# Wider w_out products and a corrected planner in a fused attention and two-expert kernel

## The chip, the cores and the metric

The kernel runs on one core of a Trainium2 chip. The metric is device time in microseconds (us), the median of three runs. Its engines are TensorE (PE in the profile; PEld is its weight load), VectorE (DVE), ScalarE (ACT), GpSimd (POOL) and SyncE (SP), whose queue starts the DMAs.

## The reference

Four batches, eight heads, 576 positions, head size 64. Keys and values are pooled into 32 memory slots by a softmax over positions; queries attend to the 32 slots. The result, 2304 tokens by 512 columns, goes through two multilayer parts.

```python
a = softmax(phi, axis=2)                       # over positions
k_m = einsum('bhsm,bhsd->bhmd', a, k)
v_m = einsum('bhsm,bhsd->bhmd', a, v)
attn = softmax(q @ k_m.T / sqrt(64))           # over the 32 slots
x = (attn @ v_m) as 2304 x 512
h = x @ w_in                                   # 512 x 2048
x = (h * sigmoid(1.702 * h)) @ w_out           # 2048 x 512
xn = x / sqrt(mean(x*x) + 1e-6) * rms_g
g = xn @ w_gate; val = xn @ w_val              # 512 x 1536 each
out = (silu(g) * val) @ w_o2                   # 1536 x 512
```

Weights of the two parts are float64; their 64-bit words are turned into float32 on the chip.

## The kernel before

**Numbers.** Every large product is made of three: high times high, low times high, high times low. The high half is a value rounded to the type fp32r that TensorE takes, the low half (made by `sub_lo`, line 680) is what the rounding left.

**Stages.** The batches form two pairs; a pair has 1152 tokens. Attention units (batch, half of the heads) make transposed scores `attnT` with the names pk, pq. The first part, "a", runs in 16 groups: 2 pairs by 8 slices of 256 hidden columns. For a group, `vm_part` (line 1017) multiplies the pooled values into w_in, so that `a_g1` (line 1055) gets the hidden columns directly from the attention weights. A step of `a_g1` covers 288 tokens; it makes two tiles `gr`, one for each 128 hidden columns: six products into a PSUM tile, the gelu on ScalarE (`gf`), a cast to the high half on ScalarE, and a subtraction for the low half on GpSimd or DVE. `a_g2` (line 1082) multiplies these by w_out: for each of four blocks of 128 output columns six products, and the sum is added into `x` by DVE (copied by ScalarE in the first group of a pair). After that come the norm (`norm_1` to `norm_4`) and the second part, "b", in 6 groups of 256 columns, with 384 tokens in a step (`b_g3` with w_gate and w_val, `b_g4` with w_o2). Loops run over groups outside and token steps inside; attention of the second pair and the norm steps are put in between as side work.

**Weights.** `w_load` (line 696) brings 1024 32-bit words a partition into one of three `raw` tiles. `w_conv` (line 714) makes float32 in a tile `pad` (part a) or `cv` (part b): an absolute value on ScalarE, a clamp (`tensor_scalar` with max and min), a shift, two merges, all on DVE unless a table says otherwise; then the cast to the high half, and the subtraction to the low half. For the second pair the float32 comes back from a cache in DRAM.

**What sets the order.** No engine's order is written by hand. All operations are recorded, and a planner (`Plan.order`, line 474) simulates the engines with a duration for every operation (`cost`, line 346) and a rate for loads (in `order`), and sends each engine's operations in the order of that simulation. Two tables bend it. `HASTE` gives a step an earlier or later due time. `OTHER` names operations of a step, by their number within it, that move from DVE to GpSimd or back. Where the simulation leaves TensorE idle, it writes products of a tile of ones (`fill`, line 557) that nobody reads; in the rows they are products with `ones_r` of 512 columns. All the recorded operations are issued at one line, 586, so rows are told apart by their tiles.

**Buffers.** Pools have a set number of buffers: `cv` 6 for float32 work, `gp` 5 for `gr`, `pp`, `sr` and `rb`, `km` 2 for `kz` and `vz`, 4 `kmT`, 8 PSUM banks. `spare` buffers are kept for the norm steps.

Of the kernel before, what the change touches and what calls it, by code (L numbers as in the profile page):

```python
# [116 lines left out]
class Plan:  # L117
# [10 lines left out]
        "a_g1 0 2 2": 34.2,  # L128
        "a_g1 0 3 0": -35.6,
        "a_g1 0 6 2": 17.9,  # L130
        "a_g1 1 3 2": 57.3,
        "a_g1 1 3 3": 40.2,
        "a_g1 1 6 3": 24.6,
        "a_g1 1 7 0": 28.0,
        "a_g1 1 7 2": 17.0,
        "a_g2 0 0 3": 35.8,
        "a_g2 0 2 3": -19.2,
        "a_g2 0 3 1": 7.7,
        "a_g2 1 0 2": 41.3,
        "a_g2 1 1 1": 41.2,  # L140
        "att_k1 3 0": 35.9,
        "att_k3 3 0": 20.5,
        "att_k4 2 1": 32.9,
        "att_k4 3 0": 7.4,
        "att_k5 1 0": 58.0,
        "att_k5 2 0": -36.4,
        "att_q1 2 0 0": 22.5,
        "att_q1 2 1 1": 15.0,
        "att_q3 2 0 0": 20.7,
        "att_q3 3 0 0": -0.9,  # L150
        "att_q3 3 1 1": 52.4,
        "att_q3s 2 1 0": -28.4,
        "att_q3s 2 1 1": 11.8,
        "att_q3s 3 0 1": 17.9,
        "att_q4 1 1 0": 54.2,
        "att_q4 2 0 1": -9.3,
        "att_q4 3 0 1": -11.3,
        "b_g3 0 2": 6.4,
        "b_g3 1 0": 34.5,
        "b_g3 1 4": -15.0,  # L160
        "b_g3 1 5": 4.6,
        "b_g4 5 4": -96.5,
        "ld_src 0 0 1": 46.6,
        "norm_2 0 2": 23.2,
        "norm_3 0 1": 22.5,
        "norm_4 0 0 2": 28.2,
        "norm_4 0 1 0": -19.0,
        "norm_4 0 1 3": 5.2,
        "norm_4 1 1 1": 26.5,
        "vm_part 0 1 1 0": 19.0,  # L170
        "vm_part 0 3 0": 18.6,
        "vm_part 0 3 1": 19.5,
        "vm_part 0 6 0": 29.2,
        "vm_part 0 7 0": 37.3,
        "vm_part 0 7 1": 17.5,
        "vm_part 1 1 0": 41.6,
        "vm_part 1 3 1": 50.7,
        "w_conv a 0 4 in 1": 40.2,
        "w_conv a 0 5 out 0": 41.1,
        "w_conv a 1 7 in 0": 67.8,  # L180
        "w_conv b 0 o2 0": 20.1,
        "w_conv b 0 val 0": 28.6,
        "w_load a 0 4 out 0": 57.5,
        "w_load b 0 o2 0": 34.1,
# [1253 lines left out]
```

## Time and profile before

| | |
|---|---|
| median of 3 runs | 885.97 us (885.95 to 886.06) |
| profiled execution | 885.36 us, of which the span from first to last instruction is 883.6 |
| TensorE busy | 865.5 us (98%), 5826 products |
| DVE, ScalarE, GpSimd busy | 553.5, 409.4, 279.6 us |
| granted TensorE clock, mean | 0.995 |
| chain that ended last | TensorE 82%, most of it products into the PSUM tiles pg (77%) |

A row of a timeline has its start, its duration, the engine, the operation, the tiles (out<-in, without buffer numbers), the shape and how many such instructions are merged; in brackets stands how long the engine was idle before, and what released it. The tiles pg hold the results of `a_g1`, `a_g2`, `b_g3` and `b_g4` alike. Products are pipelined, so the duration of a single one holds its latency; the distance between two starts is what it costs in a stream. A granted clock of 1.00 is 2.4 GHz, one of 0.5 is 1.2 GHz.

### The profile page before, as it was taken

To read this page: it belongs to the slowest core of one execution; us is meant where nothing else is said; L and a number is where in the kernel's file an instruction comes from. 1 tells how busy PE (TensorE), PEld (TensorE's weight loads), DVE (VectorE), ACT (ScalarE), POOL (GpSimd) and SP (SyncE) were. 2 spreads that over 40 slices of the span, in tenths; PEclk is the share of its full clock that TensorE was granted. 3 is DMA by queue.
4 is the path that set the end of the run, shared out by engine and by line. 5 is a ranking of instruction groups with operands and counts; after the bars stand their busy time and mean duration, and the time that the engine had idled before them with its cause. 6 is when DMAs were issued, how large, how long until landed. Compare 5 with 4: busy or idle time off the path is not lost.

```text
span 883.6 us, 14955 instructions
## 1 busy us (share of the span) xinstructions
PE 865.5 (98%) x5826; PEld 823.5 (93%) x5826; DVE 553.5 (63%) x1113; ACT 409.4 (46%) x891; POOL 279.6 (32%) x262
## 2 busy tenths in 40 slices
PE   7999989999999999999999999999999999999997
PEld 5889989999999999999999999999999999999997
DVE  4979889998964378688876563194366346333333
ACT  2687658677767656565574531231132132111110
POOL 2254565455485755664250110210021021001000
PEclk9999999999999999999999999999999999999999
DMA  9975548755411212122322040022022000000214
GB/s 237 265 183 142 154 150 228 197 143 150 117 52 42 72 30 66 50 84 75 100 69 92 0 144 1 1 74 70 1 71 73 1 1 24 1 1 1 61 48 108
DMA packets 40535, 74.64 MB, mean 84 GB/s; under 512 B 3856, under 2 KB 16144, under 8 KB 40464
## 3 DMA queue, kind: packets, MB, share of 16 engines
q1 hardware_dynamic: 40464, 73.68, 30.2%
q8 instruction: 46, 0.75, 0.4%
q14 instruction: 25, 0.20, 0.1%
HBM read 60.56 MB, written 13.11 MB: 83 GB/s over the span
## 4 chain that ended last, share of the span: by engine, by line
PE 82%; DVE 2%; DMA 1%; ACT 1%; issue 0%; DVEq 0%; SPq 0%
PE pg L586 77%; PE pvm L586 2%; PE pq L586 1%; DMA kmisc<-in_phi_dram 1%; PE pk L586 1%; DVE kmisc L586 0%; PE pnm L586 0%; DVE stage L586 0%; PE pnr L586 0%; DVE gr L586 0%; DVE x L586 0%; DVE vm_7l L586 0%; ACT L586 0%; ACT vm_6h L586 0%; DVE pad L586 0%
## 5 line engine op out<-in xcount | busy, mean ns | idle before, releaser
L586 PE MATMUL pg<-gr,a_outh 128*128 128x288 f32 x960 | 207.0, 297 | 2.8 <-POOL gr L586 1.3
L586 PEld LDWEIGHTS pg<-gr,a_outh 128*128 128x128 f32 x960 | 158.3, 188 | 4.5 <-DVE gr L586 2.3
L586 PE MATMUL pg<-gr,a_outl 128*128 128x288 f32 x480 | 141.2, 294 | 1.3 <-DVE a_outl L586 1.3
L586 PE MATMUL pg<-b_o2h,pp 128*128 128x512 f32 x432 | 140.7, 391 | 0.0
L586 DVE TENSOR_TENSOR x<-x,pg 128x288 f32<-128x288 f32 x224 | 97.8, 449 | 52.4 <-PE pg L586 50.6
L586 DVE TENSOR_TENSOR pf<-sg,pg 128x384 f32<-128x384 f32 x72 | 39.9, 554 | 144.8 <-PE pg L586 132.8
L586 ACT ACTIVATE sg<-pg 128x384 f32<-128x384 f32 x72 | 35.3, 491 | 152.1 <-PE pg L586 150.3
L586 PEld LDWEIGHTS pg<-b_o2h,pp 128*128 128x128 f32 x432 | 81.1, 188 | 16.0
L586 ACT CAST pp<-pf 128x384 fp32r<-128x384 f32 x72 | 37.0, 513 | 126.4 <-DVE pf L586 126.0
L586 POOL TENSOR_TENSOR gr<-gf,gr 128x288 fp32r<-128x288 f32 x82 | 71.2, 877 | 72.4 <-ACT gr L586 58.2
L586 POOL TENSOR_TENSOR b_o2l<-cv,b_o2h 128x512 fp32r<-128x512 f32 x10 | 12.8, 1299 | 253.4 <-ACT b_o2h L586 217.6
L586 PEld LDWEIGHTS pg<-gr,a_outl 128*128 128x128 f32 x480 | 90.2, 188 | 1.5 <-DVE a_outl L586 1.5
L586 DVE TENSOR_TENSOR oacc<-oacc,pg 128x512 f32<-128x512 f32 x90 | 61.7, 685 | 44.3 <-PE pg L586 43.8
L586 PE MATMUL pg<-b_o2l,pp 128*128 128x512 f32 x216 | 84.7, 392 | 0.0
L586 ACT ACTIVATE gf<-pg 128x288 f32<-128x288 f32 x128 | 51.9, 410 | 36.8 <-PE pg L586 35.5
L586 PE MATMUL pg<-xnh,b_gateh 128*128 128x384 f32 x288 | 62.0, 336 | 0.0
L586 PE MATMUL pg<-xnh,b_gatel 128*128 128x384 f32 x288 | 61.8, 335 | 0.0
L586 PE MATMUL pg<-xnh,b_valh 128*128 128x384 f32 x288 | 61.6, 334 | 0.0
L586 PE MATMUL pg<-xnh,b_vall 128*128 128x384 f32 x288 | 61.5, 334 | 0.0
L586 PE MATMUL pg<-xnl,b_valh 128*128 128x384 f32 x288 | 61.5, 334 | 0.0
L586 PE MATMUL pg<-xnl,b_gateh 128*128 128x384 f32 x288 | 61.5, 334 | 0.0
L586 ACT CAST gr<-gf 128x288 fp32r<-128x288 f32 x128 | 53.7, 433 | 16.7 <-PE pg L586 8.7
(210 smaller groups left out, 1777.9 us busy)
## 6 DMA issues: line engine op xcount, KB each, us to landing
raw_a_in<-in_moe_w_in_dram SPq DMA_DIRECT2D x16, 512.0 KB, 5.3
raw_a_out<-in_moe_w_out_dram SPq DMA_DIRECT2D x16, 512.0 KB, 5.0
cache<-pad SPq DMA_DIRECT2D x32, 256.0 KB, 4.9
raw_b_gate<-in_moe_w_gate_dram SPq DMA_DIRECT2D x12, 512.0 KB, 3.8
raw_b_val<-in_moe_w_val_dram SPq DMA_DIRECT2D x12, 512.0 KB, 3.7
raw_b_o<-in_moe_w_out_dram SPq DMA_DIRECT2D x12, 512.0 KB, 3.8
stage<-in_k_dram SPq DMA_DIRECT2D x8, 576.0 KB, 7.8
stage<-in_v_dram SPq DMA_DIRECT2D x8, 576.0 KB, 9.4
```

The costliest lines, as they stand in the source:

```text
L586: getattr(self.real[op.eng], op.name)(*op.args, **op.kw)
```

## The change

**w_out products.** A step of `a_g2` covers 384 tokens in place of 288, except in the first two groups of the first pair. The steps of `a_g1` keep 288 tokens, so a `gr` tile of 384 tokens is now filled by two of them: a new function, `pieces`, cuts a step of `a_g1` at the borders of the 384-token tiles. Steps 1 and 2 of a group make two pieces each, of 96 and 192 tokens, each with its own cast and its own subtraction. The loop over slots sends a step of `a_g2` one slot after the one that completed its tile.

```diff
+    def width(pr, g):
+        return HALF if (pr, g) in ((0, 0), (0, 1)) else TB
+
+    def pieces(pr, g, t):
+
+        w, a = width(pr, g), t * HALF
+        while a < (t + 1) * HALF:
+            k = a // w
+            b = min((k + 1) * w, (t + 1) * HALF)
+            yield k, a - t * HALF, b - t * HALF, a - k * w
+            a = b
...
-            gr = gpp.tile([P, 2, TB], F32R, tag="gp", name="gr")
-            A.copy(out=gr[:, 0, :HALF], in_=gf[:, :HALF])
-            sub_lo(G, gr[:, 1, :HALF], gf[:, :HALF], gr[:, 0, :HALF])
-            gt[pr, g, t, fc] = gr
+            for k, c0, c1, d0 in pieces(pr, g, t):
+                if (pr, g, k, fc) not in gt:
+                    gt[pr, g, k, fc] = gpp.tile([P, 2, TB], F32R, tag="gp", name="gr")
+                gr, d = gt[pr, g, k, fc], slice(d0, d0 + c1 - c0)
+                A.copy(out=gr[:, 0, d], in_=gf[:, c0:c1])
+                sub_lo(G, gr[:, 1, d], gf[:, c0:c1], gr[:, 0, d])
...
-                        ps[:, :HALF], lhsT=wo[a][:, fc, es], rhs=gr[fc][:, y, :HALF],
+                        ps[:, :w], lhsT=wo[a][:, fc, es], rhs=gr[fc][:, y, :w],
...
-        if prev:
-            line(a_g2 if prev[0] == "a" else b_g4, *prev[1:])
+        for step in late:
+            line(*step)
+        late = []
+        if key[0] == "b":
+            late = [(b_g4, *key[1:], t)]
+        elif width(*key[1:]) == HALF:
+            late = [(a_g2, *key[1:], t)]
+        elif t:
+            late = [(a_g2, *key[1:], t - 1)]
```

**Planner durations.** GpSimd's `tensor_scalar` gets a duration by its kind, and loads with 96 partitions (q, k, v and phi) a lower rate.

```diff
-            t = 0.15 + 0.00215 * n if two else 0.05 + 0.00104 * n
+            each = 0.00215 if two else 0.00104 if op.kw.get("op0") is ALU.mult else 0.00355
+            if op.kw.get("op") is ALU.mult:
+                each = 0.0016
+            t = 0.05 + each * n + (0.1 if two else 0.0)
...
-                bus = max(bus, t + 1.3) + n / (235e3 if x.ap[0][1] == 96 else 290e3)
+                bus = max(bus, t + 1.3) + n / (224e3 if x.ap[0][1] == 96 else 290e3)
```

**Tables.** `HASTE` and `OTHER` have new entries throughout. In the numbering of `w_conv` for part a, 1 is the clamp and 7 the subtraction:

```diff
-        "w_conv a 0 3 in 0": (1,),
-        "w_conv a 0 3 in 1": (1,),
+        "w_conv a 0 3 in 0": (7,),
+        "w_conv a 0 3 in 1": (7,),
```

**Buffers.** To make room, `rb` moves into the single buffer `kmi`, and `kz`, `vz` and `kmT` lose one each.

```diff
-    cvp = pool("cv", 6, spare=2)
+    cvp = pool("cv", 6, spare=3)
-    gpp = pool("gp", 5, spare=1)
+    gpp = pool("gp", 6)
-    kmp = pool("km", 2, strict=True)
+    kmp = pool("km", 1, strict=True)
-    ones_f = const.tile([P, P], F32, name="ones_f")
+    ones_f = const.tile([P, 1], F32, name="ones_f")
...
-        nrm[pr, t] = gpp.tile([P, TB], F32, tag="gp", name="rb")
+        nrm[pr, t] = kmiscp.tile([P, 1024], F32, tag="kmi", name="rb")[:, :TB]
```

**What moves, engine by engine.** First TensorE, in the fifth group of the first pair, the products of one PSUM tile with w_out. Before (`a_0_4_outh` and `outl` are the high and low half of w_out's slice, `gr_509` and `gr_512` the two tiles of a token step):

```order
L586 MATMUL pg2_533<-gr_509,a_0_4_outh_434 128x288
L586 MATMUL pg2_533<-gr_509,a_0_4_outl_435 128x288
L586 MATMUL pg2_533<-gr_509,a_0_4_outh_434 128x288
L586 MATMUL pg2_533<-gr_512,a_0_4_outh_434 128x288
L586 MATMUL pg2_533<-gr_512,a_0_4_outl_435 128x288
L586 MATMUL pg2_533<-gr_512,a_0_4_outh_434 128x288
```

After:

```order
L569 MATMUL pg2_517<-gr_473,a_0_4_outh_424 128x384
L569 MATMUL pg2_517<-gr_473,a_0_4_outl_425 128x384
L569 MATMUL pg2_517<-gr_473,a_0_4_outh_424 128x384
L569 MATMUL pg2_517<-gr_476,a_0_4_outh_424 128x384
L569 MATMUL pg2_517<-gr_476,a_0_4_outl_425 128x384
L569 MATMUL pg2_517<-gr_476,a_0_4_outh_424 128x384
```

A PSUM tile still takes six products, now of 384 columns, and a group makes 12 such tiles in place of 16. In all, 1440 + 96 products of 288 columns become 192 of 288 and 1008 of 384.

Second, GpSimd, in the middle of the first pair, where the weights of the groups 2 to 4 are made. Before (`TENSOR_SCALAR pad` is a clamp, `a_..outl` or `inl` with `pad` the subtraction that makes a weight's low half, `gr` the subtraction of a hidden tile):

```order
L586 TENSOR_TENSOR a_0_2_outl_299<-pad_116,a_0_2_outh_298 128x512 x2
L586 TENSOR_SCALAR pad_116<-pad_116 128x512 x3
L586 TENSOR_TENSOR gr_337<-gf_336,gr_337 128x288
L586 TENSOR_TENSOR a_0_3_inl_340<-pad_116,a_0_3_inh_339 128x512 x2
L586 TENSOR_SCALAR pad_116<-pad_116 128x512
L586 TENSOR_TENSOR gr_352<-gf_351,gr_352 128x288
```

After:

```order
L569 TENSOR_TENSOR gr_319<-gf_318,gr_319 128x288
L569 TENSOR_TENSOR gr_334<-gf_333,gr_334 128x288
L569 TENSOR_TENSOR a_0_2_outl_299<-pad_116,a_0_2_outh_298 128x512
L569 TENSOR_TENSOR gr_337<-gf_351,gr_337 128x96
L569 MEMSET kz_411 128x192
L569 TENSOR_TENSOR a_0_3_outl_364<-pad_116,a_0_3_outh_363 128x512
L569 TENSOR_TENSOR gr_349<-gf_357,gr_349 128x192
L569 TENSOR_TENSOR gr_352<-gf_360,gr_352 128x192
L569 TENSOR_TENSOR gr_358<-gf_377,gr_358 128x288
```

The clamps have left this stretch; over the whole program GpSimd has 6 of them in place of 22 and DVE 16 more. The subtractions of `gr` now have 96, 192 or 288 columns, and GpSimd has 124 of them in place of 82 (DVE 60 in place of 46).

Third, TensorE at the start, around the transposes of the first unit's queries (`pq_133` to `pq_136`), the transposes of the second unit's maxima (`pk_143`, `pk_145`) and the first scores (`pq_137`). Before:

```order
L586 MATMUL pvm<-a_0_inl,vlh_131 128x256
L586 MATMUL pq_133<-ones_r 128x512 x9
L586 MATMUL pq_133<-ident,stage_0_111 128x96 x3
L586 MATMUL pk_143<-ident,kmisc_1_112 128x96
L586 MATMUL pq_135<-ident,stage_0_111 128x96 x3
L586 MATMUL pq_134<-ident,stage_0_111 128x96 x3
L586 MATMUL pk_145<-ident,mx 96x128
L586 MATMUL pq_136<-ident,stage_0_111 128x96 x3
L586 MATMUL pq_137<-kmT_0_130,stage_0_111 96x2x32 x6
```

After:

```order
L569 MATMUL pk_143<-ones_r 128x512 x13
L569 MATMUL pk_143<-ident,kmisc_1_112 128x96
L569 MATMUL pq_133<-ident,stage_0_111 128x96 x3
L569 MATMUL pk_145<-ident,mx 96x128
L569 MATMUL pq_135<-ident,stage_0_111 128x96 x3
L569 MATMUL pq_134<-ident,stage_0_111 128x96 x3
L569 MATMUL pq_136<-ident,stage_0_111 128x96 x3
L569 MATMUL pq_137<-ones_r 128x512
L569 MATMUL pq_137<-kmT_0_130,stage_0_111 96x2x32 x6
L569 MATMUL pvm<-a_0_inh,vlh_131 128x256
```

The nine fill products in front of `pq_133` are gone, and 13 now stand in front of `pk_143`, which comes before `pq_133` instead of behind it. The `pvm` products, the last of which is the first row before, now begin behind the first scores. In the whole program the fill products go from 60 to 71, all but one of the 71 before the first products of `a_g1`.

## Rows read from the trace of the kernel before

**Rows 1.** The page: span; busy us, share, instructions of each engine

```profile
span 883.6 us, 14955 instructions
...
PE 865.5 (98%) x5826; PEld 823.5 (93%) x5826; DVE 553.5 (63%) x1113; ACT 409.4 (46%) x891; POOL 279.6 (32%) x262
```

**Rows 2.** Stretches: busy us (instructions) by engine, PEclk, DMA share, GB/s

```profile
0.00:57.00 57.00, 51.31 (x426) 42.57 (x427) 39.27 (x107) 30.24 (x78) 19.42 (x25) 0.94 1.01 248
57.00:250.00 193.00, 185.29 (x1641) 179.68 (x1640) 170.14 (x372) 138.17 (x318) 103.37 (x88) 1.00 0.56 155
250.00:425.00 175.00, 174.87 (x1344) 174.55 (x1343) 117.46 (x245) 109.77 (x248) 105.07 (x113) 1.00 0.20 60
```

**Rows 3.** Groups: TensorE's w_out products; count, busy us, mean ns, idle before

```profile
L586 PE MATMUL pg<-gr,a_outh 128*128 128x288 f32 x960 | 207.0, 297 | 2.8 <-POOL gr L586 1.3 <-DVE gr L586 1.2
...
L586 PE MATMUL pg<-gr,a_outl 128*128 128x288 f32 x480 | 141.2, 294 | 1.3 <-DVE a_outl L586 1.3
...
L586 PE MATMUL pg<-gr,wide 128*128 128x288 f32 x96 | 13.8, 296 | 0.0
```

**Rows 4.** Timeline, TensorE, 289 to 295 us: start us, us, operation, count

```profile
289.17 0.42 PE L586 MATMUL pg<-gr,a_outh 128*128 128x288 f32 x2
...
294.70 0.43 PE L586 MATMUL pg<-gr,a_outh 128*128 128x288 f32 x2
```

**Rows 5.** Timeline, TensorE, 602 to 613 us

```profile
602.63 0.85 PE L586 MATMUL pg<-xnh,b_valh 128*128 128x384 f32 x4
...
608.87 0.39 PE L586 MATMUL pg<-b_o2h,pp 128*128 128x512 f32 x1
...
612.99 0.87 PE L586 MATMUL pg<-xnh,b_gateh 128*128 128x384 f32 x4
```

**Rows 6.** Timeline, 58 to 63 us, all engines; in brackets: idle before, and releaser

```profile
58.82 1.91 POOL L586 TENSOR_SCALAR pad<-pad 128x512 f32<-128x512 f32 x1
...
60.76 0.43 DVE L586 TENSOR_SCALAR pad<-pad 128x512 uint32<-128x512 uint32 x1 [2.58 <-POOL pad L586]
...
62.81 0.40 PE L586 MATMUL pg<-gr,a_outl 128*128 128x288 f32 x1 [1.31 <-DVE a_outl L586]
```

**Rows 7.** Timeline, 101 to 107 us

```profile
101.62 4.21 POOL L586 TENSOR_SCALAR pad<-pad 128x512 f32<-128x512 f32 x2 [0.88 <-ACT pad L586]
...
106.85 0.53 PE L586 MATMUL pg<-gr,a_outh 128*128 128x288 f32 x2 [1.26 <-POOL gr L586]
```

**Rows 8.** Timeline, 124 to 129 us

```profile
124.01 0.66 ACT L586 ACTIVATE pad<-raw_a_in 128x512 f32<-128x512 f32 x1 [1.31 <-DMA raw_a_in<-in_moe_w_in_dram]
...
125.06 0.44 PE L586 MATMUL pk<-ident,kz 128*128 128x128 f32 x2 [0.99 <-ACT kz L586]
...
127.47 0.66 ACT L586 ACTIVATE pad<-raw_a_out 128x512 f32<-128x512 f32 x1 [1.45 <-DMA raw_a_out<-in_moe_w_out_dram]
...
128.44 1.23 PE L586 MATMUL pq<-kmT,stage 128*96 128x64 f32 x12 [1.25 <-ACT kmT L586]
```

**Rows 9.** Timeline, 156 to 158 us

```profile
156.66 1.91 POOL L586 TENSOR_SCALAR pad<-pad 128x512 f32<-128x512 f32 x1 [1.60 <-ACT pad L586]
156.72 0.87 DVE L586 TENSOR_TENSOR gr<-gf,gr 128x288 fp32r<-128x288 f32 x1
...
157.64 0.53 PE L586 MATMUL pg<-gr,a_outh 128*128 128x288 f32 x2 [0.84 <-DVE gr L586]
```

**Rows 10.** Groups of the three other engines: count, busy us, mean ns, idle before

```profile
L586 POOL TENSOR_SCALAR pad<-pad 128x512 f32<-128x512 f32 x22 | 43.0, 1956 | 21.8 <-ACT pad L586 21.6
...
L586 DVE TENSOR_TENSOR x<-x,pg 128x288 f32<-128x288 f32 x224 | 97.8, 449 | 52.4 <-PE pg L586 50.6 <-ACT vm_3h L586 0.3
...
L586 DVE TENSOR_SCALAR pad<-pad 128x512 f32<-128x512 f32 x10 | 5.3, 528 | 4.2 <-ACT pad L586 4.2
...
L586 ACT CAST gr<-gf 128x288 fp32r<-128x288 f32 x128 | 53.7, 433 | 16.7 <-PE pg L586 8.7 <-POOL sq L586 2.4 <-issue 1.6
```

**Rows 11.** Timeline, TensorE, 20 us: fill products before q's first transposes

```profile
20.32 3.52 PE L586 MATMUL pq<-ones_r 128*128 128x512 f32 x9
```

More of the change, by code (lines that the diff above doesn't have):

```diff
@@ L127 @@
     HASTE = {
[L128 to L184, printed above, removed]
+        "a_g1 0 1 0": 23.8,
+        "a_g1 0 5 2": 24.6,
+        "a_g1 0 7 3": 36.5,
+        "a_g2 0 1 0": 26.3,
+        "a_g2 0 1 2": 49.0,
+        "a_g2 0 1 3": 32.3,
+        "a_g2 0 4 1": 30.2,
+        "a_g2 0 4 2": 25.5,
+        "a_g2 0 5 1": 31.9,
+        "a_g2 0 6 1": 25.9,
@@ new lines @@
+        "a_g2 1 2 0": 52.5,
+        "a_g2 1 3 2": 50.1,
+        "a_g2 1 5 1": 50.3,
+        "att_k4 3 1": 31.1,
+        "att_k5 1 0": 58.9,
+        "att_k5 2 0": 18.3,
+        "att_k5 2 1": -66.5,
+        "att_k5 3 0": 32.9,
+        "att_q1 3 0 1": 7.5,
+        "att_q3 2 0 0": 20.9,
+        "att_q3 2 0 1": 30.6,
+        "att_q3s 2 0 1": 0.7,
+        "att_q3s 2 1 1": 25.3,
+        "att_q3s 3 0 0": -71.4,
+        "att_q3s 3 0 1": -42.9,
+        "att_q4 2 0 0": -6.7,
+        "att_q4 2 1 1": 21.8,
@@ new lines @@
+        "att_q4 3 0 0": -5.2,
+        "att_q4 3 0 1": -5.6,
+        "b_g4 1 0": 21.6,
+        "b_g4 5 5": 67.5,
+        "norm_1 1 1": 19.0,
+        "norm_2 1 0": 41.4,
+        "norm_3 0 1": -30.1,
+        "norm_4 0 1 0": -62.2,
+        "norm_4 0 1 1": -48.3,
+        "norm_4 0 2 1": 24.7,
+        "norm_4 0 2 2": 16.3,
+        "norm_4 1 0 2": -14.7,
+        "vm_part 0 1 0 0": 22.6,
+        "vm_part 0 3 0": 20.7,
+        "vm_part 0 3 1": 20.5,
+        "w_conv a 0 5 out 0": 59.5,
+        "w_conv a 0 6 in 1": 38.8,
@@ L185 @@
+        "w_conv b 1 gate 1": -14.2,
+        "w_load a 0 3 in 0": 50.4,
     }
     OTHER = {
[1 row of a table removed]
+        "a_g1 0 0 1": (17,),
         "a_g1 0 0 2": (17,),
[3 rows of a table removed]
+        "a_g1 0 0 3": (8, 17),
+        "a_g1 0 1 0": (8,),
+        "a_g1 0 1 1": (8, 17),
         "a_g1 0 1 2": (8, 17),
[13 rows of a table removed]
+        "a_g1 0 1 3": (17,),
+        "a_g1 0 2 0": (17,),
+        "a_g1 0 2 1": (8, 10, 21),
+        "a_g1 0 3 0": (8, 17),
+        "a_g1 0 3 1": (8, 10, 19, 21),
+        "a_g1 0 3 2": (8, 10),
+        "a_g1 0 3 3": (8,),
@@ L207 @@
+        "a_g1 0 4 0": (8, 17),
+        "a_g1 0 4 2": (8,),
+        "a_g1 0 4 3": (17,),
+        "a_g1 0 5 0": (8,),
+        "a_g1 0 5 1": (19, 21),
+        "a_g1 0 5 2": (21,),
+        "a_g1 0 5 3": (8,),
+        "a_g1 0 6 1": (10, 21),
+        "a_g1 0 6 2": (19, 21),
+        "a_g1 0 6 3": (17,),
         "a_g1 0 7 0": (17,),
[4 rows of a table removed]
+        "a_g1 0 7 1": (19,),
+        "a_g1 0 7 2": (8, 10, 19, 21),
+        "a_g1 1 2 2": (19,),
+        "a_g1 1 2 3": (8,),
         "a_g1 1 3 1": (8,),
[1 row of a table removed]
+        "a_g1 1 3 2": (19,),
@@ L214 @@
         "a_g1 1 3 3": (17,),
[10 rows of a table removed]
+        "a_g1 1 4 1": (21,),
+        "a_g1 1 4 2": (8, 10, 19),
+        "a_g1 1 5 2": (10, 19, 21),
+        "a_g1 1 5 3": (8, 17),
+        "a_g1 1 6 2": (21,),
+        "a_g1 1 7 1": (10,),
+        "a_g1 1 7 3": (8,),
         "att_k3 1 0": (2,),
[2 rows of a table removed]
+        "att_k3 1 1": (2,),
+        "att_k3 2 1": (2,),
         "att_q3s 0 1 1": (3,),
+        "att_q3s 1 0 0": (3,),
         "att_q3s 1 1 0": (3,),
[4 rows of a table removed]
+        "att_q3s 1 1 1": (3,),
+        "norm_1 0 0": (3,),
+        "norm_1 0 2": (3,),
@@ L234 @@
         "norm_1 1 0": (2,),
[6 rows of a table removed]
         "norm_4 0 2 1": (2,),
         "norm_4 0 2 2": (2,),
[4 rows of a table removed]
+        "norm_4 0 2 3": (2,),
+        "norm_4 1 0 3": (2,),
+        "w_conv a 0 0 in 0": (1, 7),
         "w_conv a 0 1 in 0": (1, 7),
         "w_conv a 0 1 out 0": (1,),
[20 rows of a table removed]
+        "w_conv a 0 1 out 1": (1, 7),
+        "w_conv a 0 2 in 0": (1,),
+        "w_conv a 0 2 in 1": (7,),
+        "w_conv a 0 2 out 0": (7,),
+        "w_conv a 0 3 in 0": (7,),
+        "w_conv a 0 3 in 1": (7,),
+        "w_conv a 0 3 out 1": (7,),
@@ L269 @@
+        "w_conv a 0 4 in 0": (7,),
+        "w_conv a 0 4 in 1": (7,),
+        "w_conv a 0 5 in 0": (7,),
+        "w_conv a 0 5 out 0": (7,),
+        "w_conv a 0 5 out 1": (7,),
+        "w_conv a 0 6 in 1": (1,),
+        "w_conv a 0 6 out 0": (7,),
+        "w_conv a 0 7 in 1": (7,),
+        "w_conv a 0 7 out 0": (7,),
+        "w_conv a 0 7 out 1": (7,),
         "w_conv a 1 0 in 0": (1,),
         "w_conv a 1 0 in 1": (1,),
[2 rows of a table removed]
+        "w_conv a 1 0 out 0": (1,),
+        "w_conv a 1 0 out 1": (1,),
@@ L273 @@
+        "w_conv a 1 1 in 0": (1,),
+        "w_conv a 1 4 in 1": (1,),
         "w_conv a 1 4 out 0": (1,),
[2 rows of a table removed]
         "w_conv a 1 5 in 1": (1,),
[3 rows of a table removed]
+        "w_conv a 1 5 out 0": (1,),
+        "w_conv a 1 6 in 0": (1,),
         "w_conv b 0 gate 0": (1, 6),
[3 rows of a table removed]
+        "w_conv b 0 o2 0": (1, 6),
+        "w_conv b 0 o2 1": (1,),
+        "w_conv b 0 val 1": (1, 6),
+        "w_conv b 1 gate 0": (6,),
+        "w_conv b 1 gate 1": (6,),
         "w_conv b 1 o2 0": (1,),
[1 row of a table removed]
     }
@@ L915, in att_k5 @@
         PE.transpose(ps[:, 256:384], vz, ident)
-        kt = kmT[u] = kmp.tile([P, 2, P], F32, tag="kmT", name=f"kmT{b}_{g}", bufs=4)
+        kt = kmT[u] = kmp.tile([P, 2, P], F32, tag="kmT", name=f"kmT{b}_{g}", bufs=3)
         A.copy(out=kt.rearrange("p a b -> p (a b)"), in_=ps[:, 0:256])
@@ L1082, in a_g2 @@
     def a_g2(pr, g, t, eng=A):
-        n = slice(t * HALF, (t + 1) * HALF)
+        w = width(pr, g)
+        n = slice(t * w, (t + 1) * w)
         if pr not in x2:
@@ L1100, in a_g2 @@
             if g == 0:
-                copy(eng, acc[:, e, n], ps[:, :HALF])
+                copy(eng, acc[:, e, n], ps[:, :w])
             else:
                 V.tensor_tensor(
-                    out=acc[:, e, n], in0=acc[:, e, n], in1=ps[:, :HALF], op=ALU.add
+                    out=acc[:, e, n], in0=acc[:, e, n], in1=ps[:, :w], op=ALU.add
                 )
-        if t == 3:
+        if t == PT // w - 1:
             wt.pop(("a", pr, g, "out"))
@@ L1249 @@
     nc.vector.memset(ones_f, 1.0)
-    nc.vector.tensor_copy(out=ones_r, in_=ones_f)
+    nc.vector.tensor_copy(out=ones_r, in_=ones_f.to_broadcast([P, P]))
     nc.vector.memset(epst, EPS)
@@ L1363 @@
     SP.dma_start(out=rg, in_=moe2_rms_g.rearrange("(e p) -> p e", p=P))
-    side, per, prev = iter(()), 2, None
+    side, per, late = iter(()), 2, []
     for j, (*key, t) in enumerate(slots):
@@ L1396 @@
                 do(step)
-        if prev:
-            line(a_g2 if prev[0] == "a" else b_g4, *prev[1:])
+        for step in late:
[7 more added lines that the diff above has]
+            late = [(a_g2, *key[1:], t - 1)]
         for step in islice(side, per + (j % 4 == 1) if j else 0):
             do(step)
-        prev = (*key, t)
     line(b_g4, NB - 1, 2 * NTB - 1)
```

75 rows, old and new, of the table OTHER are left out of this document.

## The prediction

> **What bounds the kernel now.** I read the page's first lines, then the busy time by stretches, then TensorE's timeline, and last the groups of instructions. TensorE is busy for 865.5 of 883.6 us [rows 1]. By stretches [rows 2] the reader is to see three things. From 250 us on it never stops: 174.87 of 175 us up to 425 us. From 57 to 250 us, where attention runs beside the first expert product, 7.7 of 193 us are idle (193 less 185.29), at a granted clock of 1.00, which is 2.4 GHz. Before 57 us the DMA share is 1.01, so loads set the pace there, and TensorE's 51.31 busy us hold fill products that nobody reads. So time can come from three places: fewer or shorter products anywhere, the 7.7 idle us, and the start.
>
> The sum is made against the profiled execution: a span of 883.6 us, 885.36 us in all. The median of the shown runs is 885.97, 0.6 us above it, and I add that at the end. A difference under 0.2% (1.8 us) cannot be told from none.
>
> **Term 1, the w_out products.** Before, there are 960 + 480 + 96 = 1536 of them, each 288 columns wide [rows 3]. After, the first two groups keep 2 x 96 = 192, and the other 14 groups have 3 x 4 x 6 = 72 in place of 96, 1008 in all at 384 columns. So 336 products go and no column does; what is saved is the part of a product that does not scale with columns. Durations of single products overlap and don't give it; distances between starts do. From 289.17 to 294.70 us, 42 w_out products of 288 columns follow each other [rows 4]: 5.53 / 42 = 131.7 ns, 11.7 ns over the 120 ns that 288 columns take at 2.4 GHz. No product of 384 columns with these operands is in the trace; the nearest are the gate and val products, whose stationary tile also changes every time: 36 of them from 602.63 to 608.87 us [rows 5], 6.24 / 36 = 173.3 ns, 13.3 over 160. Four narrow ones cost 526.8 ns and three wide ones 519.9, so each of the 336 exchanges is worth 6.9 ns: **2.3 us**. Bounds: if the fixed part stayed at 11.7 ns, three would cost 515.1, and the term is 3.9 us. If it were as at 512 columns (18 products from 608.87 to 612.99 us [rows 5], 228.9 ns, 15.6 over 213.3), three cost 526.8, and the term is nothing. I take 2.3, as the gate products are alike in width and in operands.
>
> On this the Trainium skill speaks against the change. The page "TensorE: Matmul & The Clock Gate", section "Back-to-back issue gap", gives the spacing of single products as columns over 2.4 GHz plus about 2.5 ns. By that fixed part the 336 products would give an estimated 0.8 us and no more. [rows 4] and [rows 5] show 11.7 and 13.3 ns in this kernel's stream, where a weight load goes with every product, so the sum keeps the rows' number.
>
> **Term 2, the waits between 57 and 250 us.** I followed the largest waits of TensorE back to what was late.
> - At 62.81 us it waited 1.31 us for a low half of w_out. DVE made that late because it had itself waited for a GpSimd clamp that ran from 58.82 for 1.91 us [rows 6].
> - At 106.85 us it waited 1.26 us for a GpSimd subtraction, queued behind two clamps that took 4.21 us from 101.62 [rows 7].
> - At 125.06 it waited 0.99 us for kz, and at 128.44 for 1.25 us for kmT. Each time ScalarE stood in its own queue before a weight tile whose load had not landed, 1.31 and 1.45 us [rows 8].
> - At 157.64 it waited 0.84 us for a subtraction that DVE ran beside a GpSimd clamp, from 156.72 for 0.87 us [rows 9].
>
> That is 5.65 of the 7.7 us. Each also costs a refill: a product's busy record is about 0.29 us where starts stand 0.13 apart, so 0.16 us of each pause shows as busy, and five waits cost about 6.4 us. Four have one of two causes. The planner books a clamp of 512 elements on GpSimd at 0.05 + 0.00104 x 512 = 0.58 us, and the trace has 1.956 [rows 10]; and it expects loads sooner than they land. These are what the diff corrects: 0.05 + 0.00355 x 512 = 1.87, and the rate for 96-partition loads falls by 5%. The rebuilt order has 6 such clamps on GpSimd in place of 22, and the stretch of GpSimd's order in the section on the change shows them gone from between the subtractions. So I expect most of the 6.4 us to go. What is late next: 2.1 us of idle time in that stretch are not of this kind and may come again anywhere, and the new order leaves as little slack as the old one. I set 2.4 us of new waits against it, about those 2.1 again: **4.0 us** gained. Bounds: all 6.4 gone, or none, with the waits only in other places.
>
> **What the change adds, and what hides it.** *DVE* gets 16 clamps of 0.528 us, 8.4 us, nearly all before 250 us, where it is busy 170.14 of 193. Its 208 additions into x become 156; if their cost went with width, 599 ns each, the total would stay at 93.4 us [rows 10]. So DVE has 22.9 idle us to hide 8.4 in, and the rival below is that they don't. *ScalarE*: 56 casts of 288 columns (433 ns, [rows 10]) become 112 pieces of 96 and 192. No row has such a piece; between nothing fixed (24 us in all, as before) and all fixed (48.5) it is 0 to 24 us more, over 14 groups. ScalarE has 55 idle us in 57 to 250 alone, so I cost it at nothing; without that cover each piece would stand in front of a w_out product. *GpSimd* loses 16 x 1.956 = 31 us of clamps and gets more and smaller subtractions. *The tiles gr* (6, all in use at times, where 5 with one kept free served) are filled by two steps of a_g1 before w_out reads them. The order covers that: a w_out product that first reads such a tile stands fewer than 30 products behind the last product that feeds it 13 of 128 times before, and 6 of 100 times after. *The single kz and vz buffers and rb in a buffer of its own* put a memset behind the transposes of the unit before; eight units in 250 us, so nothing.
>
> **Term 3, the start.** The fill products go from 60 to 71. In front of q's first transposes 9 of them took 3.52 us from 20.32 [rows 11]; now 13 stand in front of the transpose of kmisc_1, a step before, and the six products pvm have moved behind the first scores. Eleven more cost nothing if TensorE would wait for loads anyway. If they run past the landing, each costs 512 columns at 2.4 or at 1.2 GHz, 0.21 or 0.43 us, 2.3 to 4.7 us in all. The bytes loaded in front of q are the same. As loads at a DMA share of 1.01 set this stretch, I take **0**, between 2 us gained (the 3.52 us of fills may have overrun q by half) and 4.7 lost.
>
> Sum: 885.4 - 2.3 - 4.0 = 879.1; with 0.6 for the median, 879.7.
>
> **The rivals.**
> - *The waits only move.* The new tables are tuned to a model that still knows nothing of, say, DVE slowed beside GpSimd [rows 9]. Then term 1 alone is left: 885.97 - 2.3 = 883.7. For it: the order before was tuned to a model too, and 2.1 us came from what no correction touches. Against it: four of five waits have the corrected causes. Chance 0.16.
> - *Nothing changes.* The wide products have the fixed part of the 512 row, and the waits move: 886. Against it the 36 products of [rows 5]. Chance 0.07.
> - *Slower: DVE becomes the bound.* From 57 to 250 us, the 8.4 us of clamps come on an engine that is 88% busy, and two of the five waits ended on it. If its idle time is scattered in pieces too short for a clamp, TensorE waits for all of it: 885.97 - 2.3 + 8.4 = 892; at half, 887.9. It decides from the point where more than 2.3 us of the 8.4 reach TensorE and the old waits are not gone. Against it: DVE no longer sits behind GpSimd clamps. Chance 0.08.
> - *More than forecast.* Term 1 at 3.9, all 6.4 of term 2, a start shorter by 1: 874.7. Chance 0.09.
>
> My own case has 0.60, and alone it spans 876.5 to 882.5. The range takes in the upper bounds and the case of term 1 alone: 874.5 to 884.9. Faster by over 0.2%: 0.60 + 0.09 and most of 0.16, 0.82; within 0.2%: 0.10; slower: 0.08.
>
> **What would show it.** Starts of 384-wide w_out products 173 ns apart, in stretches without a pause, show term 1; 175.6 or more refute it. Term 2 is right if TensorE's idle time from 57 to 250 us falls from 7.7 to about 4 us and no wait of DVE on a GpSimd clamp of 1.9 us ends in one. If DVE's busy time there rises above 180 us and TensorE's waits name DVE, the slower rival holds. Term 3 is wrong if the first product of a_g1 starts more than 2 us away from where it starts before. A time over 884.2 or under 874.5 makes the forecast wrong.

## The result, and the profile after

| | before | after |
|---|---|---|
| median | 886.01 us (885.95 to 887.8, 4 runs) | 875.09 us (873.77 to 875.81, 4 runs) |
| profiled execution | 885.36 us | 874.62 us |

The ratio is 0.987, with a 95% interval from 0.9852 to 0.9888: 10.9 us between the medians. The direction was as forecast; the gain was 1.7 times the 6.3 us of the sum, and the time came out near the lower end of the range.

The page of the changed kernel begins with these lines, as [rows 1]:

```profile
span 872.6 us, 14373 instructions
...
PE 859.6 (99%) x5501; PEld 821.4 (94%) x5501; DVE 545.7 (63%) x1094; ACT 417.6 (48%) x947; POOL 256.7 (29%) x285
```

The stretches, as [rows 2] and with the same columns, 42 to 57 us also by itself, and that one first as it was in the kernel before:

```profile
42.00:57.00 15.00, 14.92 (x142) 13.71 (x142) 11.95 (x33) 11.89 (x34) 7.34 (x7) 0.89 0.99 235
```

```profile
0.00:57.00 57.00, 51.02 (x443) 44.17 (x444) 38.85 (x106) 30.25 (x76) 19.82 (x26) 0.97 1.02 272
42.00:57.00 15.00, 14.68 (x150) 13.98 (x151) 10.92 (x27) 11.61 (x32) 6.35 (x7) 1.00 1.06 307
57.00:250.00 193.00, 190.56 (x1573) 186.52 (x1572) 178.91 (x403) 146.40 (x357) 70.26 (x81) 1.00 0.52 150
250.00:425.00 175.00, 175.00 (x1138) 174.84 (x1137) 107.00 (x209) 109.54 (x269) 115.95 (x144) 1.00 0.21 63
```

TensorE's idle time between 57 and 250 us fell from 7.7 to 2.4 us, GpSimd's work there from 103.4 to 70.3 us, and DVE's rose from 170.1 to 178.9. What TensorE still waits for in that stretch (who waits, for whom, total us, times, longest):

```profile
PE pq L569 <- ACT stage L569: 1.3, 1, 1.3
PE pvm L569 <- DVE vll L569: 0.5, 1, 0.5
PE pg L569 <- DVE vm_0l L569: 0.4, 1, 0.4
PE pq L569 <- DVE stage L569: 0.2, 1, 0.2
```

None of them is for a tile `gr`, a half of w_out, `kz` or `kmT`, on which the five waits of [rows 6 to 9] ended. But the longest has the cause of [rows 8]: ScalarE stood before a weight tile whose load had not landed, and the copy into `stage` came behind it.

```profile
111.76 0.67 ACT L569 ACTIVATE pad<-raw_a_out 128x512 f32<-128x512 f32 x1 [1.74 <-DMA raw_a_out<-in_moe_w_out_dram]
...
113.04 1.23 PE L569 MATMUL pq<-kmT,stage 128*96 128x64 f32 x12 [1.33 <-ACT stage L569]
```

In i1_after, a later execution of the same kernel, ScalarE stood 0.56 us there and TensorE did not wait. The groups, as [rows 10]:

```profile
L569 POOL TENSOR_SCALAR pad<-pad 128x512 f32<-128x512 f32 x6 | 12.3, 2046 | 7.5 <-ACT pad L569 7.5
...
L569 DVE TENSOR_TENSOR x<-x,pg 128x384 f32<-128x384 f32 x156 | 84.0, 548 | 42.3 <-PE pg L569 40.7
...
L569 DVE TENSOR_SCALAR pad<-pad 128x512 f32<-128x512 f32 x26 | 10.9, 426 | 5.7 <-ACT pad L569 5.7
...
L569 ACT CAST gr<-gf 128x288 fp32r<-128x288 f32 (+2 forms) x184 | 60.0, 361 | 7.2 <-PE pg L569 4.8 <-PE pnm L569 0.2
```

And w_out products of 384 columns in a stretch without a pause:

```profile
285.13 0.51 PE L569 MATMUL pg<-gr,a_outh 128*128 128x384 f32 x2
...
288.77 0.51 PE L569 MATMUL pg<-gr,a_outh 128*128 128x384 f32 x2
```

The rows between count 21 products from the first start to the last: 3.64 / 21 = 173.3 ns.

**Where the time went.** For every product of 256, 288, 384 or 512 columns I took the distance to the next start. What exceeds the undisturbed distance (119.5 ns by the same reading of the products `pvm`; 131.7 [rows 4]; 173.3 and 228.9 [rows 5]) is called lost time. Small products are counted by their distances, pauses included. From the first start to the last this gives, in us:

| | before | after | difference |
|---|---|---|---|
| undisturbed distances | 776.8 | 774.5 | -2.3 |
| lost before 57 us | 4.4 | 0.9 | -3.4 |
| lost from 57 to 250 us | 14.1 | 6.7 | -7.5 |
| lost later | 3.1 | 2.9 | -0.2 |
| small products | 57.3 | 59.4 | +2.0 |
| fill products | 21.6 | 22.1 | +0.5 |
| sum | 877.3 | 866.4 | -10.9 |

The 14.1 us are 12 pauses of more than 0.16 us, 9.0 us in all, and 55 shorter ones, 4.9 us. In the changed kernel 4 long ones are left, 2.6 us, and 41 short ones, 3.5 us. So 6.4 us came from the long pauses and 1.4 from the short.

### The profile page after: what moved, and what is told of

It reads as the page before. It is cut to its first block, busy times and chain, and to the rows that moved or that the text cites. A ratio compares the mean times of both kernels' runs of the same rounds, so it can differ in the third digit from the quotient of the medians.

```text
span 872.6 us, 14373 instructions
## 1 busy us (share of the span) xinstructions
PE 859.6 (99%) x5501; PEld 821.4 (94%) x5501; DVE 545.7 (63%) x1094; ACT 417.6 (48%) x947; POOL 256.7 (29%) x285
## 4 chain that ended last, share of the span: by engine, by line
PE 90%; DVE 3%; DMA 3%; ACT 1%; issue 1%; SPq 1%; POOL 0%; DVEq 0%; ACTq 0%
PE pg L569 84%; PE pvm L569 2%; PE pq L569 2%; DMA stage<-in_q_dram 2%; DVE stage L569 1%; PE pk L569 1%; DMA raw_a_out<-in_moe_w_out_dram 1%; DVE pad L569 1%; SPq L569 1%; PE pnm L569 0%; DVE vm_0l L569 0%; ACT stage L569 0%; ACT pad L569 0%; DVE vm_1l L569 0%; PE pnr L569 0%
## 5 line engine op out<-in xcount | busy, mean ns | idle before, releaser
L569 PE MATMUL pg<-gr,a_outh 128*128 128x384 f32 (+1 forms) x736 | 195.5, 333 | 0.0
L569 PEld LDWEIGHTS pg<-gr,a_outh 128*128 128x128 f32 x736 | 132.9, 188 | 0.1
L569 PE MATMUL pg<-gr,a_outl 128*128 128x384 f32 (+1 forms) x368 | 122.0, 332 | 0.0
L569 DVE TENSOR_TENSOR x<-x,pg 128x384 f32<-128x384 f32 (+1 forms) x172 | 90.9, 539 | 42.9 <-PE pg L569 41.1
L569 POOL TENSOR_TENSOR gr<-gf,gr 128x288 fp32r<-128x288 f32 (+2 forms) x124 | 79.3, 656 | 105.5 <-ACT gr L569 73.5
L569 POOL TENSOR_TENSOR b_o2l<-cv,b_o2h 128x512 fp32r<-128x512 f32 x11 | 14.6, 1346 | 239.1 <-ACT b_o2h L569 239.1
L569 PEld LDWEIGHTS pg<-gr,a_outl 128*128 128x128 f32 x368 | 69.1, 188 | 0.0
L569 ACT CAST gr<-gf 128x288 fp32r<-128x288 f32 (+2 forms) x184 | 60.0, 361 | 7.2 <-PE pg L569 4.8
```

Source lines behind the costliest of these rows:

```text
L569: getattr(self.real[op.eng], op.name)(*op.args, **op.kw)
```

## The experiments

The theory: clamps on GpSimd, booked at 0.58 us where they take 1.96, made most of the lost time; at the right durations the planner keeps them out of the way. Rivals: the wide products carry more than their 2.3 us; the newly searched tables do it, whatever the durations; the eleven added fill products shorten the start; the corrected load rate does it. Between them, experiments that hold the order tell more than those that plan anew, so they come first. "Held" means that the recorded order is sent as it is, and only what is named runs on another engine, is left out or is cut.

**The clamps, with the order held.** In f1_clamps_back the changed kernel's order is kept and the 22 clamps of the old table run on GpSimd again; as two of the changed kernel's own six are among them, GpSimd has 26 in all. In f2_clamps_dve the order of before is kept and its 22 clamps run on DVE, so that GpSimd has none.

```diff
             for _, _, op in self.order():
-                getattr(self.real[op.eng], op.name)(*op.args, **op.kw)
+                eng = op.eng
+                if getattr(op, "key", None) in self.MOVED:   # clamps of the 22 steps
+                    eng = "POOL"                             # f2: "DVE"
+                getattr(self.real[eng], op.name)(*op.args, **op.kw)
```

f1_clamps_back, expected: 

> The changed kernel in its own order, word for word, with the clamps that the old table gave to GpSimd run there again, each at the place where it stands on DVE. Theory A, clamps on GpSimd make waits because subtractions that TensorE needs queue behind 1.96 us each: 3 to 6 us more than the changed kernel, 878 to 881 us, with waits of TensorE on GpSimd or on DVE behind pad. Rival B, DVE gains what GpSimd loses and TensorE does not notice: 875 us.

f2_clamps_dve, expected: 

> The kernel before in its own order, with its 22 clamps of the first part's weights run on DVE at the same places. Theory A, three of the five large waits go (3.4 us and their refills): 881 to 883 us. Rival B, DVE is 88% busy and 11.6 us more of it take the place of the waits: 886 us or more.

f1_clamps_back took 886.32 us, ratio 1.0017 (0.9992 to 1.0042): the whole gain of 11 us is gone, more than the theory had set. f2_clamps_dve took 879.7, ratio 0.9943 (0.9924 to 0.9963), a gain of 5.8 us and somewhat more than its theory's 881 to 883. The stretch from 57 to 250 us, of f1_clamps_back and then of f2_clamps_dve:

```profile
57.00:250.00 193.00, 184.83 (x1509) 177.69 (x1508) 169.14 (x359) 140.17 (x348) 98.17 (x90) 1.00 0.53 147
```

```profile
57.00:250.00 193.00, 189.09 (x1674) 184.55 (x1674) 175.38 (x396) 139.42 (x320) 73.95 (x76) 1.00 0.56 157
```

TensorE's idle time is 8.2 us with the clamps on GpSimd (lost time 14.1) and 3.9 without them (lost time 9.2). That f1_clamps_back lost the same 14.1 us as the kernel before is a coincidence: its longest waits are others than the five of [rows 6 to 9], as this order was made for clamps on DVE.

```profile
PE pg L597 <- DVE vm_4l L597: 1.8, 1, 1.8
PE pg L597 <- DVE gr L597: 1.5, 1, 1.5
PE pk L597 <- DVE kmisc L597: 1.5, 1, 1.5
```

How one clamp reaches TensorE can be read from the timeline of f1_clamps_back:

```profile
99.51 3.80 POOL L597 TENSOR_SCALAR pad<-pad 128x512 f32<-128x512 f32 x2
...
101.46 0.82 DVE L597 TENSOR_SCALAR pad<-pad 128x512 uint32<-128x512 uint32 x1 [1.49 <-POOL pad L597]
...
103.34 0.43 DVE L597 TENSOR_SCALAR pad<-pad 128x512 uint32<-128x512 uint32 x1 [1.06 <-POOL pad L597]
...
104.05 0.68 DVE L597 TENSOR_TENSOR gr<-gf,gr 128x288 fp32r<-128x288 f32 x1
...
104.79 1.19 PE L597 MATMUL pg<-gr,wide 128*128 128x288 f32 x7 [1.55 <-DVE gr L597]
```

Two clamps take 3.80 us. DVE stands 1.49 and 1.06 us before the shifts of their two tiles; behind these its queue holds the subtraction for `gr`, and TensorE waits 1.55 us for that. In the changed kernel the two clamps of the same place run on DVE, with the two shifts right behind them (one row for all four, 1.43 us), and the products after them follow without a wait:

```profile
98.51 1.43 DVE L569 TENSOR_SCALAR pad<-pad 128x512 f32<-128x512 f32 x4
```

f2_clamps_dve also answers a question on the loads. At the place of [rows 8], in the order of before, nothing about its loads was changed, and yet TensorE waits for neither `kz` nor `kmT`. First the kernel before at that place, then f2_clamps_dve:

```profile
113.45 1.92 POOL L586 TENSOR_SCALAR pad<-pad 128x512 f32<-128x512 f32 x1 [1.74 <-ACT pad L586]
...
115.41 1.02 DVE L586 TENSOR_SCALAR pad<-pad 128x512 uint32<-128x512 uint32 x1 [1.32 <-POOL pad L586]
...
117.98 1.91 DVE L586 SCALAR_TENSOR_TENSOR pad<-raw_a_out,pad 128x512 uint32<-128x512 uint32 x2
...
119.13 0.38 SPq L586 DMA_DIRECT2D raw_a_in<-in_moe_w_in_dram  x1
...
120.14 0.35 SPq L586 DMA_DIRECT2D raw_a_out<-in_moe_w_out_dram  x1
```

```profile
111.05 1.28 DVE L614 SCALAR_TENSOR_TENSOR pad<-raw_a_out,pad 128x512 uint32<-128x512 uint32 x2
...
112.20 0.38 SPq L614 DMA_DIRECT2D raw_a_in<-in_moe_w_in_dram  x1
...
113.21 0.36 SPq L614 DMA_DIRECT2D raw_a_out<-in_moe_w_out_dram  x1
...
116.57 0.67 ACT L614 ACTIVATE pad<-raw_a_in 128x512 f32<-128x512 f32 x1 [1.03 <-DMA raw_a_in<-in_moe_w_in_dram]
...
117.78 0.38 PE L614 MATMUL pk<-ident,kz 128*128 128x128 f32 x2
118.48 0.68 ACT L614 ACTIVATE pad<-raw_a_out 128x512 f32<-128x512 f32 x1
...
119.60 1.15 PE L614 MATMUL pq<-kmT,stage 128*96 128x64 f32 x12
```

A load is issued when a merge on DVE has read the `raw` tile that it overwrites. In the kernel before that merge stands behind a shift that waited 1.32 us for a GpSimd clamp. From ScalarE's first reading of the tile before (112.70 and 107.08 us) to the first of the two loads it takes 6.4 us there and 5.1 with the clamp on DVE, so the clamp made the loads some 1.3 us late. The rest is the loads' own: from issue to reading the first took 4.9 us before and 4.4 here, the second 7.3 and at most 5.3, and no run here says why. With both, ScalarE's first wait shrinks from 1.31 to 1.03 us, the second (1.45 us) is gone, and neither reaches TensorE. So clamps and loads were not wholly two causes there: the late load was in part a clamp's doing. A load rate corrected by itself, with the clamps left, was not tried.

**The six clamps that stayed.** h1_six holds the changed kernel's order and runs its last six GpSimd clamps on DVE (the same edit, other steps). It was run a second time as i2_six, beside the changed kernel itself, i1_after, on one chip.

h1_six, expected: 

> The changed kernel with its order of instructions held, the six clamps that it still has on GpSimd run on VectorE. Theory A (at the right durations these six were placed where they cost nothing): 874.5 to 876 us, no change to be measured. Rival B (a GpSimd clamp of 1.9 us is a cost wherever it stands): 873.5 to 874.3 us, 0.1 to 0.2 us less for each.

i1_after, expected: 

> The changed kernel as it is, run on one chip with the next one, so that the two can be told apart. Theory B (each of the six clamps left on GpSimd costs something): 873.8 to 876 us. Theory A (they cost nothing, and the 2.8 us between the changed kernel and its copy without them were a difference of chips): the same time as the next kernel to within 1 us.

i2_six, expected: 

> The changed kernel's order with its six GpSimd clamps on VectorE, a second time. Theory B: 871.5 to 873.5 us, 1.5 to 3.5 us below the run beside it, with TensorE's lost time between 57 and 250 us about 1.2 us lower. Theory A: within 1 us of it.

h1_six took 872.33 us, ratio 0.9836 (0.9802 to 0.987), below the bands of both theories, which looked like a gain. Side by side it was none: i1_after 874.29 us, ratio 0.9862 (0.9839 to 0.9886), and i2_six 876.11, ratio 0.9879 (0.9851 to 0.9907), 1.8 us more where theory A had allowed 1. The lost time from 57 to 250 us is 5.5, 5.4 and 5.6 us in the three. So the six cost nothing there that these runs can show: what costs is a clamp on GpSimd at a place for which the order was not made. The 3.8 us between h1_six and i2_six, one program on two chips, are not explained: the kernel before took 886.35 and 886.03 us on the same two. In the two profiled executions, of 873.12 and 879.21 us, what differs is the start: the first product of `a_g1` stands at 44.3 and 50.5 us. From 24 to 36 us, h1_six and then i2_six:

```profile
24.00:36.00 12.00, 11.16 (x144) 10.47 (x143) 11.02 (x30) 8.81 (x25) 6.14 (x6) 1.00 1.08 306
```

```profile
24.00:36.00 12.00, 12.00 (x104) 11.29 (x101) 7.39 (x22) 5.45 (x12) 3.96 (x4) 0.52 1.00 289
```

**The fills, and the width.** f5_nofill is the changed kernel's order without its 71 fill products. f7_split cuts four of every six of its 384-wide w_out products into two of 192.

```diff
+                if isinstance(op, Fill):      # f5
+                    continue
...
+                if step[:4] == "a_g2" and 384 columns and not (start or stop):   # f7, in words
+                    for c in (slice(0, 192), slice(192, 384)): matmul(out[:, c], rhs[:, c])
```

f5_nofill, expected: 

> The changed kernel in its own order without the 71 fill products. Theory A, the fills stand only in waits for loads and keep the granted clock up: without them the clock of the first 57 us falls below 0.9 and the kernel takes 1 to 4 us more, 876 to 879 us. Rival B, fills that run past a landing delay the start: 873 us or less.

f7_split, expected: 

> The changed kernel in its own order with four of the six 384-column w_out products of each PSUM tile (all but the first and the last) cut into two of 192 columns: 672 products more and no column more. Theory A, a product costs its columns and 12 to 13 ns: 8 to 9 us more, 883 to 884 us. Rival B, by the Trainium skill's page on TensorE the fixed part is about 2.5 ns: 1.7 us more, 877 us. Rival C, with 192 columns the weight load of each product no longer hides: more than 20 us more.

f5_nofill took 879.89 us, ratio 0.9943 (0.9922 to 0.9964), 4.8 us above the changed kernel, a little over theory A's 879; the clock of the first 57 us fell to 0.91, not below 0.9. It shows why fills pay where TensorE waits for loads anyway:

```profile
36.00:42.00 6.00, 2.77 (x21) 1.95 (x19) 5.97 (x19) 3.00 (x7) 3.39 (x2) 1.00 1.07 256
42.00:48.00 6.00, 3.63 (x20) 3.58 (x19) 5.82 (x14) 2.02 (x4) 0.83 (x1) 0.51 1.08 239
```

From 36 to 42 us the changed kernel with its fills has this:

```profile
36.00:42.00 6.00, 5.36 (x25) 3.69 (x23) 6.00 (x20) 2.61 (x7) 1.90 (x2) 1.00 1.07 258
```

Without them TensorE is busy for 2.77 of 6 us, and after that the granted clock stands at 0.51, which is nearly all at 1.2 GHz. Its first product of `a_g1` starts at 47.9 us in place of 44.0. The fills as a whole are worth some 5 us; that the eleven added ones matter was not shown.

f7_split took 906.19 us, ratio 1.0247 (1.0217 to 1.0277): 31 us for 672 more products, 46 ns each, and no column more. Theory A's 8 to 9 us and rival B's 1.7 are both far off; the size is that of rival C, but that the weight load is the reason was not tested. Its timeline:

```profile
285.80 0.36 PE L573 MATMUL pg<-gr,a_outl 128*128 128x192 f32 x2
286.00 0.61 PE L573 MATMUL pg<-gr,a_outh 128*128 128x192 f32 x4
286.45 0.38 PE L573 MATMUL pg<-gr,a_outl 128*128 128x192 f32 x2
286.67 0.36 PE L575 MATMUL pg<-gr,a_outh 128*128 128x384 f32 x1
```

Eight products take 0.87 us, 109 ns each, 29 over the 80 ns that 192 columns take at 2.4 GHz. At 288 and 384 columns it was 11.7 and 13.3 over. So the part that does not scale with columns is not one number, and the 6.9 ns that an exchange of four 288-wide for three 384-wide products is worth can't be carried on to narrower ones.

**Planned anew.** Five kernels let the planner work again: e1_narrow is the changed kernel with all w_out products 288 wide (its table entries for pieces of a step then name whole steps); e2_costs is the kernel before with the corrected durations and its old tables; e3_clamps is the kernel before with the 22 clamps on DVE by its table, at the old durations; e4_oldcosts is the changed kernel with the old durations. g1_searched is the kernel before with the corrected durations and tables searched anew for just that.

```diff
 def width(pr, g):                                   # e1
-    return HALF if (pr, g) in ((0, 0), (0, 1)) else TB
+    return HALF
...
-            t = 0.15 + 0.00215 * n if two else 0.05 + 0.00104 * n     # e2, g1 (e4: the reverse)
+            each = 0.00215 if two else 0.00104 if op.kw.get("op0") is ALU.mult else 0.00355
+            t = 0.05 + each * n + (0.1 if two else 0.0)               # and the loads' rate, 224e3
...
-        "w_conv a 0 ...": (1, ...),                 # e3: entry 1 out of 22 lists of OTHER
+        "w_conv a 0 ...": (...),
```

e1_narrow, expected: 

> The changed kernel with all w_out products 288 columns wide again, its buffers, durations and tables kept (an entry for a piece of a step now moves that step's whole subtraction). Theory A, the products are worth only their spacing: 336 products more at 6.9 ns, 2.3 us, about 877.4 us, and TensorE idle from 57 to 250 us stays near 2.4 us. Rival B, the wider steps are also what removed the waits: 880 us or more, with idle time there back above 5 us.

e2_costs, expected: 

> The kernel before with the corrected durations alone, its own tables and its 288-column products kept. Theory A, wrong durations made the waits: the planner now sees 1.9 us clamps and later loads and orders around them, 4 to 6 us less than before, 880 to 882 us. Rival B, the gain is in the tables that were searched with the right durations: old tables with new durations give 886 us or more.

e3_clamps, expected: 

> The kernel before with all 22 clamps of the first part's weights on DVE, by the table; its durations and products kept. Theory A, clamps on GpSimd that the planner books at a third of their time made three of the five large waits (3.4 us of idle time): 882 to 883 us. Rival B, DVE becomes the bound between 57 and 250 us, where it is 88% busy, and 22 x 0.53 us more of it reach TensorE in part: 888 to 892 us. Rival C, the order shifts at random and the waits only move: 885 to 887 us.

e4_oldcosts, expected: 

> The changed kernel with the old durations for GpSimd and loads, its tables and wide products kept. Theory A, the order needs right durations: the waits come back, 879 to 881 us. Rival B, with 6 clamps left on GpSimd the durations hardly matter any more: 875 to 876 us.

g1_searched, expected: 

> The kernel before with its 288-wide products and its buffers, the planner's durations for GpSimd and loads corrected, and its tables of numbers searched anew for exactly that (so neither the old tables nor those of the changed kernel). Theory A (the corrected durations with tables that fit them carry the gain, the width gives only the 2.3 us of its products): 877 to 880 us, ratio 0.990 to 0.993; TensorE's lost time between 57 and 250 us at 7 to 10 us in place of 14, its 288-wide products at 131.7 ns. Rival B (the wider products are what makes a good order possible): 883 us or more, lost time there of 12 us or more.

| | us | ratio | lost 57 to 250 us | fills after 57 us |
|---|---|---|---|---|
| e1_narrow | 889.66 | 1.0049 (1.0029 to 1.0069) | 7.4 | 14, 3.8 us |
| e2_costs | 897.07 | 1.0131 (1.0105 to 1.0157) | 14.2 | 49, 11.9 us |
| e3_clamps | 890.08 | 1.0051 (1.003 to 1.0072) | 11.5 | 12, 6.0 us |
| e4_oldcosts | 884.89 | 0.9984 (0.9964 to 1.0004) | 10.2 | 26, 6.4 us |
| g1_searched | 882.94 | 0.9966 (0.9941 to 0.9992) | 8.6 | 2, 1.2 us |

Correcting the durations without new tables made the kernel 11 us slower. Where fills stand, the planner itself foresaw a pause of TensorE; e2_costs has them between 57 and 250 us (groups of that stretch):

```profile
L589 PE MATMUL pg<-ones_r 128*128 128x512 f32 x34 | 8.3, 386 | 0.8 <-DVE x L589 0.8
L589 PE MATMUL pq<-ones_r 128*128 128x512 f32 x15 | 3.4, 381 | 0.0
```

The kernel before has none after 57 us and lost 14.1 us there: its planner saw no pause long enough for a fill where there were several. e1_narrow and e3_clamps misled: I expected one edit, and got a new order from tables that no longer fit it. e3_clamps lies in the band of its rival B, but not by that rival's cause: DVE is busy for 170.8 us from 57 to 250, as before (170.1); the fills after 57 us are new, and the granted clock from 24 to 36 us was 0.55 in its profiled execution, where the kernel before had 0.99. In e1_narrow TensorE's idle time from 57 to 250 us stays at 2.6 us, as its theory A had it, so the wide products are not what removed the waits there; but the loss has moved behind 250 us, where TensorE is busy for only 168.44 of 175 us, with one wait of 6 us:

```profile
PE pg L569 <- ACT gf L569: 6.0, 1, 6.0
```

e4_oldcosts shows the other half: the new tables and the wide products without the corrected durations give next to nothing, a smaller gain than either of its theories had. g1_searched came out 3 us above the theory's band and just below the rival's 883, while its lost time of 8.6 us is the theory's and not the rival's. It loses elsewhere, as at 12.58 us, where TensorE has stood 3.75 us:

```profile
12.58 2.72 PE L1107 MATMUL pk4s<-ones_f,e 96*128 96x1 f32 x12 [3.75 <-ACT e L1107]
```

A shorter search than the one behind the changed kernel may be the reason, or the 384-wide steps may leave a planner more room; this stays open. None of the five beats the changed kernel.

## Why the prediction was too small

- **Term 1, the w_out products: right in the spacing.** 173.3 ns was taken and 173.3 measured; the undisturbed distances, which are the spacings times the counts, fell by the 2.3 us. No run shows the 2.3 us as a time by itself. The fixed part of 2.5 ns that the Trainium skill gives ("TensorE: Matmul & The Clock Gate", section "Back-to-back issue gap") would have made it 0.8. The section calls that formula the isolated gap of a single product, and says that it misses in a stream where a weight load goes with every product; so it did not really speak against the change, and the rows, which are such a stream, differ from it.
- **Term 2, the waits: right in kind, too small.** The step that failed is "I set 2.4 us of new waits against it". By distances the five waits cost 6.5 us, as the prediction's 6.4 had it, and the long pauses fell by 6.4 in all: the five are gone, the other long ones came again at the same size (2.5 us before, 2.6 after), and no new waits came on top. The short pauses gave 1.4 us more. They are no part of the prediction, since a pause shorter than the 0.16 us that a product's busy record overhangs doesn't show as idle at all. Measured, this term is 7.5 us of lost time in place of 4.0, or 5.5 if all that the small products gained in length is held against it, though 1.1 of these 2.0 us belong to products of one column before 57 us. That clamps on GpSimd make such waits is shown both ways: f2_clamps_dve took 4.9 us of lost time away from the order of before, and f1_clamps_back put 7.5 into the new one.
- **Loads as a second cause: the step "These are what the diff corrects" was wrong.** The rate that the diff lowers is that of loads with 96 partitions, and the late loads of [rows 8] bring weight tiles of 128 partitions, whose rate is unchanged. They were late in part because of clamps, as f2_clamps_dve shows. In the changed kernel ScalarE still stands before such loads, up to 3.5 us, and once, at 113.04 us, TensorE waits 1.33 us for what comes after, over half of the idle time that is left in that stretch.
- **Term 3, the start: the step "I take 0" failed.** 3.4 us less is lost before 57 us in this execution, and 2.2 less in i1_after (2.1 us lost, against 4.4). The sign set for a refutation, the first product of `a_g1`, hardly moved (43.4 to 44.0 us) and was the wrong one: the first w_out product moved from 60.7 to 53.1 us. From 42 to 57 us the kernel before ran at a granted clock of 0.89, the changed one at 1.00. Part of this may be how the clock falls in one execution: h1_six and i2_six differ by 3.8 us with one program. Over the executions on record that part is small. The ten of the kernel before with a mean granted clock of 0.998 average 884.6 us, the four of the changed kernel with the same mean clock 874.4, so about 10 of the 11 us are there at an equal mean clock. What in the order makes the rest of the start's gain, no run separates.
- **Costs put at nothing: right.** DVE went to 178.9 us, under the 180 set as the mark of the slower rival, and is named in waits of 1.1 us. A clamp on DVE takes 426 ns, not 528, and a wide addition into x 548, not 599. The 56 more casts add 6.3 us to ScalarE's busy time (53.7 to 60.0), and no wait of TensorE from 57 to 250 us is for a `gr`.
- **The rival "More than forecast", 874.7 us at a chance of 0.09,** came nearest to the time, but by other terms: it had 3.9 for term 1, 6.4 for term 2 and 1 for the start, and 2.3, 7.5 and 3.4 were measured, with 2.5 us of longer small and fill products against them. That its sum fits is luck.

Of the 11 us, 2.3 are the width by its spacing, and 5 to 6 the clamps in the order of before; the rest came with the new order. With the clamps back on GpSimd that order keeps nothing of the gain. The parts do not add up, because each order was made for its own clamps.

## What to carry to other kernels

Measure what an engine loses by distances between starts, not by idle time, before pricing its waits: here 14.1 us against 7.7, a third of it in pauses too short to show as idle. Where a planner sets the order, look first for operations whose booked duration is far from the trace's, as 0.58 against 1.96 us; correct them and search the tables again, since here either without the other gave nothing or cost 11 us. Then check that the correction touches the operations that were late: here the corrected load rate did not. To test one cause in such a kernel, hold the order and change the one thing, and run kernels that differ by less than 0.5% together and more than once: one program took 872.3 and 876.1 us here.
